# Attention inside a fused kernel: small vector operations rewritten as sums beside a constant, gates moved to other factors, one copy moved to VectorE, and a new order of the rounds

## The chip, the core and the metric

The kernel runs on one core of a Trainium2 chip. A core has TensorE for matrix products and transpositions (PE in the profile; PEld is its loading of weights), VectorE (DVE), ScalarE (ACT), GpSimd (POOL) and a queue (SP) that issues most of the DMA transfers. The metric is the time of one execution in microseconds, the median over several runs.

## The reference

Three stages follow one another: an attention with a memory, a dense layer with a layer norm inside, and a gated dense layer. Only the first is changed.

```python
# B, H, S, D = 4, 8, 576, 64
scores = q @ k.T / sqrt(D), causal; scores -= scores.max(-1)
a = np.exp(scores); a /= a.sum(-1, keepdims=True) + 1e-09
local = a @ v
q_p = phi(q)                       # phi(x) = (x if x > 0 else exp(x) - 1) + 1
mem_ret = q_p @ M_prev
mem_norm = (q_p @ z_prev)[..., None] + 1e-06
g = 1 / (1 + exp(-beta))           # one gate per head
attn = g * mem_ret / mem_norm + (1 - g) * local
# then, over 2304 tokens:
x = layer_norm(softmax-gated(attn @ w_in)) @ w_out      # _moe_ref
out = (sigmoid(x @ w_gate) * (x @ w_val)) @ w_out2      # _moe2_ref
```

## The kernel before

The attention works on 16 pairs of heads (4 batches, 4 pairs each, so that two heads of width 64 fill 128 partitions). The 576 rows of a pair are four blocks of 128 and a tail of 64, which for both heads together makes a fifth block; so a pair has nine row groups (two heads in each of four blocks, and the tail), and its transformed q has ten columns of 64.

One pair goes through these steps, which the text calls by the names of their methods:

- `lq`, `lk`, `lv`, `lz`: loads of q, k, v with M, and z. `tq_p`, `tk_p`: q and k are transposed on TensorE; `tq_h`, `tk_h` (ScalarE) round them to a high part and `tq_l`, `tk_l` (VectorE) form the rest.
- `ph_e` (ScalarE), `ph_m` (VectorE, lines 306 and 307), `ph_g` (GpSimd, line 311, writes `G`), `ph_r` (VectorE, lines 321 to 323, writes `nr`), `ph_s` (GpSimd, line 328): phi(q), its product with z, the sums of ten blocks of 64 as normalisers, and phi(q) divided by them. `tf_p` and `tf_c` transpose the result and copy it out.
- `s0` to `s4`: for each block `s_p` (TensorE, scores), `s_m` (VectorE, line 378, mask and row maximum), `s_e` (ScalarE, line 386, exponential, which also writes the row sums). `n01_r`, `n23_r`, `n4_r` (VectorE, lines 390 and 391, write `rs`) invert the row sums, and `n0_p` to `n4_p` (GpSimd, line 395) multiply the rows by them.
- `g0`, `g1`, `t0` to `t3`, `tt`, `tc`: transpositions of the probabilities (`_p`, TensorE) and copies out of PSUM (`_c`). `x0_m`, `a00`, `a01` and `x1_m`, `a10` to `a14`: the products that give the output, copied into `X` by `x0_c` and `x1_c`.

Beside each pair a sixteenth of the first dense layer's weights, which come as 64-bit numbers, is converted: `cv_a` (VectorE, lines 108 and 109), `cv_r` (ScalarE), `cv_b` (VectorE, lines 117 and 122), `cv_p` (GpSimd, line 502), `cv_h` (ScalarE), `cv_l` (VectorE, line 510).

The order is written out by hand in `ORDER`: one round runs through the whole list, and `name:d` means that round i does this step for pair i+d. Within an engine the instructions stand in that order; between engines only data and buffers make one wait for another. Score tiles in PSUM share two buffers, as do the transposed probabilities. The second and third stage are ordered by a scheduler, not by this list.

The gates enter twice before the change: `g10` holds 1 + exp(-beta), by which the normalisers are multiplied before they are inverted, and `o9` holds 1/(1-g), by which the row sums are multiplied before they are inverted.

Of the kernel before, what the change touches and what calls it, by code (L numbers as in the profile page):

```python
# [22 lines left out]
tk_p:1 cv_a:-1 tq_h:1 n01_r:0 ph_g:1 tq_l:1 t1_p:-1 tk_h:1 cv_r:-1 t2_p:-1 tk_l:1 t2_c:-1 n0_p:0 t1_c:-1 cv_b:-1
n4_r:0 x0_m:-1 a01:-1 a00:-1 x1_m:-1 a14:-1 a13:-1 a12:-1 a11:-1 a10:-1 s0_p:1 s3_e:0 n1_p:0 s1_p:1 ph_r:1 s2_e:0
cv_p:-1 n4_p:0 s0_m:1 lq:3 lv:0 cv_h:-1 s1_m:1 s2_p:1 n23_r:0 s3_p:1 g0_p:0 tt_p:0 lk:3 ph_s:1 s2_m:1 lz:3 cv_d:0
s4_p:1 x1_c:-1 s0_e:1 s1_e:1 tt_c:0 g0_c:0 s3_m:1 tf_p:1 x0_c:-1 tc_p:0 g1_p:0
# [831 lines left out]
```

## Time and profile before

| What | Value |
|---|---|
| median of three runs | 920.97 us (920.97 to 921.63) |
| the profiled execution | 921.52 us, of which 919.7 us are the span shown |
| PE busy over the span | 870.2 us (95%) |
| DVE busy | 578.1 us (63%) |
| ACT busy | 423.8 us (46%) |
| POOL busy | 260.1 us (28%) |

The attention takes about the first 243 us. The shares are averages over stages that differ: a stage is read from its own windows and timelines. Times in a timeline row are the start in us and the busy time in us; a number in brackets is the idle time of that engine just before and what ended it. Where rows are merged (x4), the busy time is that of the group.

### The profile page before, as it was taken

Reading aid. Unit: us, or ns where it says so; the run is one execution under the profiler, and the core shown is the slowest. Engines: PE = TensorE matmul, PEld = TensorE weight load, DVE = VectorE, ACT = ScalarE, POOL = GpSimd, SP = SyncE. Lnnn points to the kernel's source line nnn. Section 1 sums busy time; section 2 is a strip of 40 time slices with the busy share of each in tenths; the row PEclk is TensorE's granted clock in tenths of the full one; section 3 lists DMA queues with packets and bytes.
Section 4 is the critical chain, followed back from the end, with each engine's and each line's share of the span. In section 5 each row is a group of like instructions: output and inputs, shape, how many; then the busy total and the mean of one; then the engine's idle time right before and its main releaser. Section 6 shows DMA issues by size and latency. Waiting matters only on the chain.

```text
span 919.7 us, 13972 instructions
## 1 busy us (share of the span) xinstructions
PE 870.2 (95%) x5224; PEld 723.4 (79%) x5224; DVE 578.1 (63%) x1321; ACT 423.8 (46%) x941; POOL 260.1 (28%) x320
## 2 busy tenths in 40 slices
PE   3799898998988999999999999999999999999998
PEld 3566666666667999999988888888888888888887
DVE  5899999999596755574924248456339735232324
ACT  2788988897676654554435233112122212111111
POOL 2566656666574211111400033012014203000000
PEclk9899999999998999999999999999999999999999
DMA  4333433442122100020300013002002300000113
GB/s 89 87 93 93 108 85 90 104 94 83 47 68 69 47 18 29 24 69 1 114 25 1 1 46 109 29 17 76 1 1 92 91 1 1 1 1 1 46 46 115
DMA packets 76292, 48.63 MB, mean 53 GB/s; under 512 B 62656, under 2 KB 62656, under 8 KB 76224
## 3 DMA queue, kind: packets, MB, share of 16 engines
q1 hardware_dynamic: 75024, 47.44, 18.6%
q8 instruction: 41, 0.67, 0.3%
q10 hardware_dynamic: 1200, 0.30, 0.2%
q14 instruction: 27, 0.22, 0.1%
HBM read 43.00 MB, written 4.72 MB: 52 GB/s over the span
## 4 chain that ended last, share of the span: by engine, by line
PE 69%; ACT 15%; DVE 7%; POOL 5%; issue 3%; DMA 1%; SPq 0%; POOLq 0%; DVEq 0%; ACTq 0%
PE gv L736 32%; PE po L755 16%; PE po L654 9%; PE h L603 7%; ACT p L386 6%; POOL p L395 3%; ACT Bt L135 2%; ACT q L280 1%; PE pl L642 1%; ACT E L300 1%; ACT kh L135 1%; ACT f L135 1%; PE sc L356 1%; PE x L465 1%; DVE exwo L109 1%
## 5 line engine op out<-in xcount | busy, mean ns | idle before, releaser
L742 DVE TENSOR_TENSOR sg<-sg,gv 128x512 f32<-128x512 f32 (+1 forms) x60 | 38.0, 633 | 176.8 <-ACT sg L741 176.8
L741 ACT ACTIVATE sg<-gv 128x512 f32<-128x512 f32 (+1 forms) x60 | 33.2, 554 | 234.6 <-PE gv L736 234.6
L736 PE MATMUL gv<-xx,gh 128*128 128x512 f32 (+1 forms) x480 | 136.1, 368 | 0.2 <-ACT xx L138 0.2
L736 PE MATMUL gv<-xx,vh 128*128 128x512 f32 (+1 forms) x480 | 136.0, 368 | 0.0
L654 PE MATMUL po<-lnT,woh 128*128 128x256 f32 x576 | 106.5, 287 | 0.3 <-ACT X L658 0.3
L736 PEld LDWEIGHTS gv<-xx,gh 128*128 128x128 f32 x480 | 87.4, 188 | 16.1 <-issue 0.4
L736 PEld LDWEIGHTS gv<-xx,vh 128*128 128x128 f32 x480 | 87.1, 189 | 14.9
L654 PEld LDWEIGHTS po<-lnT,woh 128*128 128x128 f32 x576 | 91.7, 194 | 1.4 <-ACT X L658 0.5
L736 PE MATMUL gv<-xx,gl 128*128 128x512 f32 (+1 forms) x240 | 88.3, 368 | 0.0
L736 PE MATMUL gv<-xx,vl 128*128 128x512 f32 (+1 forms) x240 | 88.3, 368 | 0.0
L386 ACT ACTIVATE p<-p,nm 128x128 f32<-128x128 f32 (+2 forms) x144 | 83.0, 585 | 7.0 <-DVE nm L378 7.0
L395 POOL TENSOR_SCALAR p<-p,rs 128x128 f32<-128x128 f32 (+2 forms) x144 | 78.5, 563 | 20.0 <-DVE rs L391 13.3
L755 PE MATMUL po<-oh,GVxs 128*128 128x512 f32 x216 | 84.1, 389 | 0.0
L755 PE MATMUL po<-ol,GVxs 128*128 128x512 f32 x216 | 84.1, 389 | 0.0
L755 PE MATMUL po<-oh,GVe 128*128 128x512 f32 x216 | 84.0, 389 | 0.0
L654 PE MATMUL po<-lnT,wol 128*128 128x256 f32 x288 | 81.8, 285 | 0.0
L603 PE MATMUL h<-wih,xs 128*128 128x512 f32 x288 | 80.6, 393 | 0.0
L762 DVE TENSOR_TENSOR X<-X,po 128x512 f32<-128x512 f32 x90 | 61.3, 684 | 22.9 <-PE po L755 22.9
L603 PEld LDWEIGHTS h<-wih,xs 128*128 128x128 f32 x288 | 53.0, 188 | 10.6 <-issue 0.5
L356 PE MATMUL sc<-kh,q 64*128 64x128 f32 (+3 forms) x256 | 37.2, 376 | 25.2 <-DVE nm L378 17.9
L142 POOL TENSOR_SCALAR gh<-exg 128x512 fp32r<-128x512 f32 x12 | 8.9, 749 | 183.0 <-PE gv L736 142.1
L138 ACT CAST GVxs<-sg 128x512 fp32r<-128x512 f32 (+1 forms) x60 | 34.8, 580 | 46.5 <-DVE sg L742 46.5
(355 smaller groups left out, 1802.2 us busy)
## 6 DMA issues: line engine op xcount, KB each, us to landing
rawg<-in_moe_w_gate_dram SPq DMA_DIRECT2D x12, 512.0 KB, 3.8
rawv<-in_moe_w_val_dram SPq DMA_DIRECT2D x12, 512.0 KB, 3.9
rawo<-in_moe_w_out_dram SPq DMA_DIRECT2D x12, 512.0 KB, 3.5
out_dram<-X SPq DMA_DIRECT2D x18, 256.0 KB, 2.0
qt<-in_q_dram SPq DMA_DIRECT2D x32, 128.0 KB, 2.8
vt<-in_v_dram SPq DMA_DIRECT2D x32, 128.0 KB, 2.9
raw<-in_moe_w_in_dram SPq DMA_DIRECT2D x16, 256.0 KB, 3.6
rawwo<-in_moe_w_out_dram SPq DMA_DIRECT2D x8, 512.0 KB, 3.5
```

The costliest lines, as they stand in the source:

```text
L135: (nc.scalar.copy if COPY[key] == "s" else nc.vector.tensor_copy)(dst, src)
L138: nc.scalar.copy(hi, src)
L356: nc.tensor.matmul(ps[:, hh, :w], q2[sl, c, w - P : w], kk[sl, :w], start=m == 0, stop=m == 2)
L386: nc.scalar.activation(p, p, AF.Exp, bias=nm, scale=-1.0, accum_out=r["sum"][:, c : c + 1])
L395: nc.gpsimd.tensor_scalar(p, p, r["rs"][:, c : c + 1], 1.0, ALU.mult, ALU.mult)
L603: nc.tensor.matmul(ph[:, j * 512 : j * 512 + 512], xs[:, s, c], w[:, j * 512 : j * 512 + 512], start=(c == 0 and s == 0 and w is hi), stop ...
L654: nc.tensor.matmul(po[:, :GW], w[:, m * P : m * P + P], L[:, x, c], start=(c == 0 and n == 0), stop=(c == NF1 - 1 and n == 2),)
L736: nc.tensor.matmul(ps[:, j, :w], wt[:, c, fs], xx[:, x, c], start=(c == 0 and n == 0), stop=(c == NC - 1 and n == 2),)
L741: nc.scalar.activation(sg[:, :w], ps[:, 0, :w], AF.Sigmoid)
L742: nc.vector.tensor_mul(sg[:, :w], sg[:, :w], ps[:, 1, :w])
L755: nc.tensor.matmul(po, GV[x][:, f, sl], wt[:, f], start=(f == 0 and n == 0), stop=(f == NCH - 1 and n == 2),)
L762: nc.vector.tensor_add(acc[:, t], acc[:, t], po)
```

## The change

Four things are changed in the attention.

1. `G` becomes one fixed tile with 65 columns for each of the ten blocks; the 65th holds 1e-6, so that one reduction gives normaliser plus constant, and the operation on line 322 that added 1e-6 and multiplied by the gate is gone. The row sums likewise go to a fixed tile with a second column of 1e-9, and the operation on line 390 becomes a reduction over two columns.
2. The gates become factors: g multiplies in `tf_c` as the scale of a ScalarE activation, and 1-g is the second factor of the GpSimd multiplication in `n_p`, whose second factor was the constant 1.0. The tables `g10` and the inverse of `o9` are not built any more.
3. `x1_c`, a copy of 128x320 elements out of PSUM, goes from ScalarE to VectorE.
4. `ORDER` is new, k of the first pair comes over the SP queue like the others (before, over ScalarE's queue), and beta is loaded first of all, one round earlier.

```diff
-s4_m:0 n3_p:-1 tq_p:1 ph_e:1 tf_c:0 tc_c:-1 g1_c:-1 t3_p:-1 s4_e:0 n2_p:-1 cv_l:-2 t0_p:-1 ph_m:1 t3_c:-1 t0_c:-1
...
+t3_c:-1 tq_p:1 n1_p:0 t0_c:-1 x1_c:-2 lq:2 tq_h:1 cv_a:-1 t2_p:-1 t1_p:-1 ph_m:1 t2_c:-1 s4_e:0 tk_p:1 ph_g:1
...
-COPY = dict(tf="s", tc="v", tt="s", kh="s", x0="v", x1="s", g0="s", g1="v", t0="s", t1="s", t2="s", t3="s")
+COPY = dict(tc="v", tt="s", kh="s", x0="v", x1="v", g0="s", g1="v", t0="s", t1="s", t2="s", t3="s")
...
+            self.G = sb.tile([P, 10, D + 1], F32, tag="G", name="G")
+            nc.vector.memset(self.G[:, :, D:], 1e-6)
+            self.sum = [sb.tile([P, 9, 2], F32, tag=f"sum{n}", name=f"sum{n}") for n in range(2)]
+            for t in self.sum:
+                nc.vector.memset(t[:, :, 1:], 1e-9)
...
-            nc.vector.tensor_scalar(bt, bt, 1.0, 1e30, ALU.add, ALU.min)
+            nc.vector.tensor_scalar_add(bt, bt, 1.0)
+            nc.vector.reciprocal(bt, bt)
             bth = bt.rearrange("p (a h) -> p a h", h=2)
-            self.g10 = sb.tile([P, HP, 10], F32, tag="g10", name="g10")
-            for c in range(NB + 1):
-                nc.vector.tensor_copy(self.g10[:, :, 2 * c : 2 * c + 2], bth)
-            nc.vector.reciprocal(bt, bt)
...
-            nc.vector.tensor_scalar_max(self.o9, self.o9, 1e-30)
-            nc.vector.reciprocal(self.o9, self.o9)
...
-            self.load_qk(n, self.kt[n % 2], k, nc.sync.dma_start if n else nc.scalar.dma_start)
+            self.load_qk(n, self.kt[n % 2], k)
...
-            nc.vector.reduce_sum(nr, r["G"].rearrange("p (c d) -> p c d", d=D), axis=AX.X)
-            nc.vector.scalar_tensor_tensor(nr, nr, 1e-6, self.g10[:, pairs[n][1]], ALU.add, ALU.mult)
+            nc.vector.reduce_sum(nr, self.G, axis=AX.X)
             nc.vector.reciprocal(nr, nr)
...
-            copy("tf", r["f"], r["fps"])
+            hp = pairs[n][1]
+            nc.scalar.mul(r["f"], r["fps"], self.gp[:, hp : hp + 1])
...
-            rs, sm, o9 = (x[:, c0:c1] for x in (r["rs"], r["sum"], self.o9[:, pairs[n][1]]))
-            nc.vector.scalar_tensor_tensor(rs, sm, 1e-9, o9, ALU.add, ALU.mult)
+            rs = r["rs"][:, c0:c1]
+            nc.vector.reduce_sum(rs, self.sum[n % 2][:, c0:c1], axis=AX.X)
             nc.vector.reciprocal(rs, rs)
...
-                nc.gpsimd.tensor_scalar(p, p, r["rs"][:, c : c + 1], 1.0, ALU.mult, ALU.mult)
+                og = self.o9[:, pairs[n][1], c : c + 1]
+                nc.gpsimd.tensor_scalar(p, p, r["rs"][:, c : c + 1], og, ALU.mult, ALU.mult)
...
-                if it == -1:
+                if it == -2:
                     self.gates_load()
```

VectorE's order in a round in the middle of the attention, from the last row maximum of pair 7 (tile `p_119`) to the first use of pair 8's q. `wil` is the weight conversion's last step, `ex` and `raw` belong to its first, `X` is the output, `E` is phi(q), `C` and `A` are transposed probabilities. Before:

```order
L378 ISA p_119,nm<-sc_4_1670,mask 128x576
L378 ISA nm 128x1
L135 COPY C_1719<-t6d 128x128
L135 COPY A_1686<-t6a_1702 128x2x128
L510 TENSOR_TENSOR wil_77<-ex_1531,wih_76 128x256
L306 TENSOR_SCALAR E_1715<-E_1715 128x640
L307 SCALAR_TENSOR_TENSOR E_1715<-qt_92,E_1715 128x640
L108 TENSOR_SCALAR ex_1744<-raw_1668 128x256
L109 TENSOR_SCALAR ex_1744<-raw_1668 128x256
L390 SCALAR_TENSOR_TENSOR rs_1679<-sum_1678,o_200 128x4
L391 RECIPROCAL rs_1679<-rs_1679 128x4
```

Here lines 306 and 307 come first and lines 108 and 109 directly behind them. After the change, around the same place:

```order
L388 TENSOR_REDUCE rs_1605<-sum_126 128x4
L389 RECIPROCAL rs_1605<-rs_1605 128x4
L135 COPY C_1675<-t6d 128x128
L509 TENSOR_TENSOR wil_77<-ex_1501,wih_76 128x256
L377 ISA p_119,nm<-sc_4_1680,mask 128x576
L377 ISA nm 128x1
L135 COPY X<-x_1_1545 128x5x64
L108 TENSOR_SCALAR ex_1713<-raw_1657 128x256
L109 TENSOR_SCALAR ex_1713<-raw_1657 128x256
L306 TENSOR_SCALAR E_1694<-E_1694 128x640
L307 SCALAR_TENSOR_TENSOR E_1694<-qt_92,E_1694 128x640
```

Lines 108 and 109 now stand ahead of lines 306 and 307, not behind them; the copy of 128x5x64 into `X` stands here; and the inversion of the row sums of blocks 0 and 1 has moved ahead of the last maximum.

GpSimd's order over one whole round, beginning with the product that writes `G`. Before:

```order
L311 TENSOR_TENSOR G_1324<-E_1287,zm_599 128x640
L395 TENSOR_SCALAR p_0_1186<-p_0_1186,rs_1251 128x128 x2
L395 TENSOR_SCALAR p_1_1200<-p_1_1200,rs_1251 128x256 x2
L502 TENSOR_TENSOR ex_1316<-ex_1316 128x256
L395 TENSOR_SCALAR p_119<-p_119,rs_1251 128x576
L328 TENSOR_TENSOR E_1287<-E_1287,nr_1391 128x640
L395 TENSOR_SCALAR p_3_1260<-p_3_1260,rs_1251 128x512 x2
L395 TENSOR_SCALAR p_2_1235<-p_2_1235,rs_1251 128x384 x2
```

Here the row groups of blocks 0 and 1 follow the product, and those of blocks 3 and 2 close the round. After:

```order
L310 TENSOR_TENSOR G<-E_1272,zm_778 128x10x64
L394 TENSOR_SCALAR p_119<-p_119,rs_1185,o_196 128x576
L394 TENSOR_SCALAR p_0_1172<-p_0_1172,rs_1185,o_196 128x128 x2
L501 TENSOR_TENSOR ex_1291<-ex_1291 128x256
L326 TENSOR_TENSOR E_1272<-E_1272,nr_1372 128x640
L394 TENSOR_SCALAR p_3_1221<-p_3_1221,rs_1185,o_196 128x512 x2
L394 TENSOR_SCALAR p_2_1200<-p_2_1200,rs_1185,o_196 128x384 x2
L394 TENSOR_SCALAR p_1_1390<-p_1_1390,rs_1395,o_196 128x256 x2
```

The row groups of blocks 3, 2 and 1 (`p_3`, `p_2`, `p_1`) now stand directly ahead of the product that writes `G`, and the tail's group and block 0 directly behind it.

On TensorE the transposition of phi(q) (`tf_p`) now stands ahead of the tail's scores (`s4_p`), so that these use the PSUM buffer of the fourth block's scores and wait for its maximum. In the second stage the scheduler's order differs too at its beginning: the first transposition of that stage's results (line 642) stood behind three row tiles' products on line 603 and now stands behind three and three quarters; the second stood two more tiles later and now stands a quarter of a tile later.

## Rows read from the trace of the kernel before

**Rows 1.** Windows: busy us (count) of PE, PEld, DVE, ACT, POOL; clock, DMA share, GB/s.

```profile
120.00:140.00 20.00, 17.98 (x163) 12.48 (x162) 19.55 (x62) 18.50 (x53) 13.16 (x20) 1.00 0.43 99
300.00:400.00 100.00, 100.00 (x673) 92.14 (x673) 62.62 (x137) 55.63 (x97) 17.18 (x21) 1.00 0.12 38
```

**Rows 2.** Timeline of DVE, one round: start, busy, line, operation, tiles.

```profile
119.64 1.66 DVE L109 TENSOR_SCALAR ex<-raw 128x256 int32<-128x256 int32 x1
...
124.18 0.80 DVE L321 TENSOR_REDUCE nr<-G 128x10 f32<-128x640 f32 x1
125.02 0.60 DVE L322 SCALAR_TENSOR_TENSOR nr<-nr,g 128x10 f32<-128x10 f32 x1
...
126.84 0.48 DVE L390 SCALAR_TENSOR_TENSOR rs<-sum,o 128x4 f32<-128x4 f32 x1
...
129.60 0.42 DVE L135 COPY X<-x 128x256 f32<-128x256 f32 x1
...
133.08 1.66 DVE L109 TENSOR_SCALAR ex<-raw 128x256 int32<-128x256 int32 x1
```

**Rows 3.** Timeline of POOL, the same round.

```profile
119.60 1.55 POOL L311 TENSOR_TENSOR G<-E,zm 128x640 f32<-128x640 f32 x1 [2.84 <-DVE E L307]
121.76 1.64 POOL L395 TENSOR_SCALAR p<-p,rs 128x128 f32<-128x128 f32 x4 [0.60 <-DVE rs L391]
124.15 0.73 POOL L502 TENSOR_TENSOR ex<-ex 128x256 f32<-128x256 f32 x1 [0.75 <-DVE rs L390]
124.86 0.75 POOL L395 TENSOR_SCALAR p<-p,rs 128x576 f32<-128x576 f32 x1
126.05 1.26 POOL L328 TENSOR_TENSOR E<-E,nr 128x640 f32<-128x640 f32 x1 [0.44 <-DVE nm L378]
127.71 2.50 POOL L395 TENSOR_SCALAR p<-p,rs 128x512 f32<-128x512 f32 x4 [0.40 <-ACT p L386]
```

**Rows 4.** Timeline of DVE: three of these operations at other times.

```profile
17.63 0.17 DVE L322 SCALAR_TENSOR_TENSOR nr<-nr,g 128x10 f32<-128x10 f32 x1
...
25.45 0.15 DVE L390 SCALAR_TENSOR_TENSOR rs<-sum,o 128x4 f32<-128x4 f32 x1
...
229.52 0.29 DVE L109 TENSOR_SCALAR ex<-raw 128x256 int32<-128x256 int32 x1
```

**Rows 5.** Timeline of PE, the same round.

```profile
126.29 0.62 PE L356 MATMUL sc<-kh,q 64*128 64x384 f32 x4 [0.84 <-DVE nm L378]
...
128.72 0.51 PE L347 MATMUL sc<-kh,q 128*128 128x288 f32 x2
...
129.47 0.30 PE L347 MATMUL sc<-kl,q 128*128 128x288 f32 x1
...
133.00 1.15 PE L417 MATMUL t7b<-ident,p 128*128 128x128 f32 x8 [0.26 <-ACT Bt L135]
```

**Rows 6.** Timeline of ACT, the same round.

```profile
125.96 0.42 ACT L135 COPY X<-x 128x320 f32<-128x320 f32 x1
...
129.00 0.59 ACT L135 COPY Bt<-t7c 128x512 f32<-128x512 f32 x1 [0.85 <-PE t7c L431]
...
130.66 0.74 ACT L300 ACTIVATE E<-qt 128x640 f32<-128x640 f32 x1 [0.58 <-POOL p L395]
```

**Rows 7.** Timeline of ACT, the beginning.

```profile
10.42 0.21 ACT L302 ACTIVATE bt<-bt 128x8 f32<-128x8 f32 x1 [2.53 <-DMA bt<-in_beta_dram]
```

**Rows 8.** Timeline of DVE, the beginning.

```profile
15.38 0.17 DVE L801 TENSOR_SCALAR gl<-gl 128x8 f32<-128x8 f32 x1 [1.23 <-DMA gl<-in_moe_g_ln_dram]
```

**Rows 9.** Timeline of POOL: `G` of pairs 2 and 15.

```profile
38.96 1.55 POOL L311 TENSOR_TENSOR G<-E,zm 128x640 f32<-128x640 f32 x1 [4.86 <-DVE E L307]
...
214.78 1.55 POOL L311 TENSOR_TENSOR G<-E,zm 128x640 f32<-128x640 f32 x1 [2.83 <-DVE E L307]
```

**Rows 10.** Timeline of PE, the two longest waits of the second stage's beginning.

```profile
262.76 1.09 PE L642 MATMUL pl<-ident,e 128*128 128x128 f32 x8 [2.32 <-ACT e L625]
...
280.66 1.12 PE L642 MATMUL pl<-ident,e 128*128 128x128 f32 x4 [3.82 <-DVE lnT L139]
```

More of the change, by code (lines that the diff above doesn't have):

```diff
@@ L21 @@
 ORDER = """
-s4_m:0 n3_p:-1 tq_p:1 ph_e:1 tf_c:0 tc_c:-1 g1_c:-1 t3_p:-1 s4_e:0 n2_p:-1 cv_l:-2 t0_p:-1 ph_m:1 t3_c:-1 t0_c:-1
[L23 to L26, printed above, removed]
+t3_c:-1 tq_p:1 n1_p:0 t0_c:-1 x1_c:-2 lq:2 tq_h:1 cv_a:-1 t2_p:-1 t1_p:-1 ph_m:1 t2_c:-1 s4_e:0 tk_p:1 ph_g:1
+tk_h:1 tq_l:1 cv_r:-1 n4_r:0 tk_l:1 t1_c:-1 n4_p:0 x0_m:-1 a01:-1 a00:-1 x1_m:-1 a14:-1 a13:-1 a12:-1 a11:-1 a10:-1
+lv:0 s0_p:1 s2_e:0 s1_p:1 g1_p:0 ph_r:1 n0_p:0 s3_e:0 cv_b:-1 x0_c:-1 s0_m:1 lk:2 s1_m:1 s0_e:1 s2_p:1 cv_p:-1
+g1_c:0 n23_r:0 lz:2 s2_m:1 s3_p:1 g0_p:0 ph_s:1 s1_e:1 g0_c:0 s3_m:1 tt_p:0 n3_p:0 n2_p:0 cv_d:0 tf_p:1 t3_p:0
+tt_c:0 n01_r:1 cv_h:-1 tc_p:0 tc_c:0 cv_l:-1 tf_c:1 s4_p:1 t0_p:0 s4_m:1 ph_e:2
 """.split()
-COPY = dict(tf="s", tc="v", tt="s", kh="s", x0="v", x1="s", g0="s", g1="v", t0="s", t1="s", t2="s", t3="s")
+COPY = dict(tc="v", tt="s", kh="s", x0="v", x1="v", g0="s", g1="v", t0="s", t1="s", t2="s", t3="s")
 CVL = "v"
@@ L215, in gates, with load_qk @@
             nc.vector.tensor_scalar(self.o9[:, :, 8], self.gp, -1.0, 1.0, ALU.mult, ALU.add)
-            nc.vector.tensor_scalar_max(self.o9, self.o9, 1e-30)
-            nc.vector.reciprocal(self.o9, self.o9)
         def psum(self, shape, name, tag="s"):
             return self.ps.tile(shape, F32, tag=tag, name=name, bufs=2)
-        def load_qk(self, n, t, src, dma=nc.sync.dma_start):
+        def load_qk(self, n, t, src):
             b, hp = pairs[n]
             for hh in range(2):
-                dma(
+                nc.sync.dma_start(
                     t[:, : 8 * D].rearrange("p (c h d) -> p c h d", h=2, d=D)[:, :, hh],
@@ L229, in load_qk @@
                 )
-            dma(
+            nc.sync.dma_start(
                 t[0:64, 8 * D : 10 * D].rearrange("p (h d) -> p h d", h=2),
@@ L309, in ph_g @@
         def ph_g(self, n, r):
-            r["G"] = self.sb.tile([P, 10 * D], F32, tag="G", name=f"G{n}")
             nc.gpsimd.tensor_mul(
-                r["G"].rearrange("p (c x) -> p c x", x=P),
-                r["E"].rearrange("p (c x) -> p c x", x=P),
-                r["z"].unsqueeze(1).to_broadcast([P, NB + 1, P]),
+                self.G[:, :, :D].rearrange("p (c h) d -> p c h d", h=2),
+                r["E"].rearrange("p (c h d) -> p c h d", h=2, d=D),
+                r["z"].rearrange("p (h d) -> p h d", h=2).unsqueeze(1).to_broadcast([P, NB + 1, 2, D]),
             )
@@ L381, in s_e @@
         def s_e(self, n, r, i):
-            if "sum" not in r:
-                r["sum"] = self.sb.tile([P, 9], F32, tag="sum", name=f"sum{n}", bufs=2)
+            if "rs" not in r:
                 r["rs"] = self.sb.tile([P, 9], F32, tag="rs", name=f"rs{n}", bufs=2)
             for (_, _, _, p, c), nm in zip(self.parts(r, i), r["m", i]):
-                nc.scalar.activation(p, p, AF.Exp, bias=nm, scale=-1.0, accum_out=r["sum"][:, c : c + 1])
+                nc.scalar.activation(p, p, AF.Exp, bias=nm, scale=-1.0, accum_out=self.sum[n % 2][:, c, 0:1])
         def n_r(self, n, r, c0, c1):
-            rs, sm, o9 = (x[:, c0:c1] for x in (r["rs"], r["sum"], self.o9[:, pairs[n][1]]))
-            nc.vector.scalar_tensor_tensor(rs, sm, 1e-9, o9, ALU.add, ALU.mult)
+            rs = r["rs"][:, c0:c1]
+            nc.vector.reduce_sum(rs, self.sum[n % 2][:, c0:c1], axis=AX.X)
             nc.vector.reciprocal(rs, rs)
```

## The prediction, made before the changed kernel had run

> **What bounds the kernel now.** I read the windows by stage first, then the timelines of one round on VectorE, GpSimd, TensorE and ScalarE side by side. In the middle of the attention VectorE is busy 19.55 of 20 us, TensorE 17.98, ScalarE 18.50; from 300 us on TensorE is busy all of the time and VectorE 63% [rows 1]. So a small VectorE operation can only matter in the attention, where it is worth its time once per round. A round lasts 13.44 us, from line 109 at 119.64 to line 109 at 133.08 [rows 2], and VectorE has no gap in it that the timeline marks.
>
> But three of its busy times are not work. Line 109 takes 1.66 us here and 0.29 us at 229.52; line 322 takes 0.60 and at 17.63 only 0.17; line 390, for blocks 2 and 3, takes 0.48 and at 25.45 only 0.15 [rows 2, 4]. Each ends when a GpSimd operation ends: line 109 at 121.30, `G` at 121.15; line 322 at 125.62, the tail's group at 124.86 + 0.75 = 125.61; line 390 at 127.32, phi(q) times its normaliser at 126.05 + 1.26 = 127.31 [rows 2, 3]. The hold costs 1.37 + 0.43 + 0.33 = 2.13 us per round, and VectorE's own work is 13.44 - 2.13 = 11.31 us. The reduction on line 321 reads one tensor and takes 0.80 us.
>
> The Trainium skill gives this hold as a rule (SBUF — State Buffer, Who interferes with whom): a VectorE instruction with two SBUF inputs, or in a two-port mode, and a GpSimd instruction exclude one another for a whole instruction, while `tensor_reduce` on trn2 never contends. The three pairs of ends agree with the first half; that a reduction is never held the trace does not show for two columns. By the rule the new reductions are free of the hold; without it they would keep 0.43 + 0.33 us.
>
> **The change part by part.** *Line 322 goes*: 0.17 us of work, and 0.43 of hold. *Line 390 becomes a reduction over two columns*, three times a round. No row shows one so small; the reduction of 640 elements at 0.80 us is the bound above, 0.15 us the nearest row by size [rows 2, 4]. I take 0.15, that is no change in work, and 0.33 of hold gone; it could be 0.15 dearer each, or 0.1 cheaper. The longer row of `G` (650 for 640) is 0.01 us.
>
> *`x1_c` moves to VectorE*: the copy of 256 columns takes 0.42 us there [rows 2], so 320 take between 0.42 and 0.53; I take 0.45. It leaves ScalarE, where it took 0.42 [rows 6]. VectorE's work is then 11.31 - 0.17 + 0.01 + 0.45 = 11.60 us.
>
> *The new order* decides the 1.37 us of line 109. Before, it stands right behind line 307, whose end releases `G` on GpSimd, and so meets `G` in every round. Now it stands ahead of line 306, at a time when GpSimd should have finished the row groups of block 1 and waits for line 307: the hold is gone. GpSimd has the room: 1.55 + 1.64 + 0.73 + 0.75 + 1.26 + 2.50 = 8.43 us of work in a round [rows 3]. But holds can appear elsewhere: lines 117 and 122 now come when GpSimd multiplies block 0, and line 510 when it multiplies blocks 2 and 1. Each can cost at most the rest of one such operation, 0 to 0.75 us [rows 3]; I take 0.3 for all. A second term: the tail's scores now wait for block 3's maximum. They take 128.72 to 129.47 + 0.30 = 1.05 us on TensorE [rows 5], and VectorE has meanwhile only an inversion, the copy of `C` and line 510 before it needs them. I take 0.3 us of wait, between 0 and 1.05. That makes 11.60 + 0.3 + 0.3 = 12.2 us.
>
> What is late next: TensorE is busy 17.98/20 x 13.44 = 12.1 us of a round [rows 1], with waits of 0.84 and 0.26 in it [rows 5]; ScalarE has gaps of 0.85 and 0.58 [rows 6], so 13.44 - 1.43 = 12.0 us of work, less 0.42 for the copy, 11.6. Three engines within half a microsecond of each other will miss some handshakes; I add 0.2 and take a round of 12.4 us, with 11.9 and 13.0 as ends. The gate as a scale in `tf_c` and the second per-partition factor in `n_p` I cost at nothing: both fall on engines with some slack, ScalarE 0.8 us and GpSimd 4 us a round. Where that cover is gone is rival E.
>
> `G` of pair 2 starts at 38.96 and of pair 15 at 214.78 [rows 9]: 13 rounds. They save 13 x (13.44 - 12.4) = 13.5 us. The round after that is bound by VectorE for some three quarters: 0.8.
>
> *The start.* beta is loaded after two pairs' q and k before; ScalarE waits 2.53 us for it, with the rounding of q queued behind [rows 7], and that wait goes. VectorE waits 1.23 us for `gl` ahead of the first normalisers [rows 8]; the scheduler now puts this after the row maxima of pair 0, so it goes too, or shrinks. Seven small operations that built `g10` and inverted `o9` go, at some 0.17 each [rows 4, 8] 1.2 us. Against these 5.0 us: beta's issue stands ahead of q's, and k of the first pair comes behind q on one queue, where its rounding waits for that of q anyway. I take 4.0, between 1 and 5.
>
> *The second stage* keeps its work; its order at the beginning differs. TensorE waits there 2.32 and 3.82 us before transpositions [rows 10]. The first one gets three quarters of a row tile of products ahead of it, which covers its wait; the second comes much sooner after it and should wait longer. I take 0, with 4 us either way.
>
> Sum: 13.5 + 0.8 + 4.0 = 18.3 us. The profiled execution has 921.52 us: 921.5 - 18.3 = 903.2. The median of the runs is 0.55 below it, less than a third of a per cent, so I say **903 us**.
>
> **The rivals.** *B, the holds only change place.* The new rows of GpSimd meet lines 117, 122 and 510, and perhaps line 109 again if block 1 runs late. Speaking for it: GpSimd works 8.43 us of every round and VectorE still has eight operations a round that it can hold. Against it: the longest meeting, with `G`, is taken apart by the order. Then a round is 13.0: 14 x 0.44 + 4 = 10 us, 911 us. The skill's sentence "Issue order, not op shape, decides who blocks" (same page and section) is this rival's rule; the ends above agree, since the same line takes 0.29 or 1.66.
>
> *C, more is gained.* If the tail's wait and the new holds both come to nothing, VectorE's 11.6 and TensorE's 12.1 less what hides in it allow 11.9: 14 x 1.54 + 5 = 26.6 us, 895 us. Against it: the two waits have their places in the order.
>
> *D, the round does not change.* If ScalarE's chain of copies and exponentials, 11.6 us without any wait, meets two waits as long as today's, 1.43, and the held 0.3 on top, a round is 13.3 again. Only the start remains, and up to that much can be lost in the second stage: 917 to 921, here 920.
>
> *E, slower.* GpSimd's multiplication gets a second per-partition factor where a constant stood; the trace has no such form. The nine of a round take 1.64 + 0.75 + 2.50 = 4.89 us [rows 3]. If each cost twice that, GpSimd would work 13.3 us, and its waits at handovers, 0.60 + 0.75 + 0.44 + 0.40 = 2.19 [rows 3], come on top: 15.5 us a round, 14 x 2.1 - 4 = 25 us more, 946 us. It decides from 13.44 - 8.43 - 2.19 = 2.8 us on, that is from 58% dearer. Against it: the first factor is per partition already.
>
> **How the numbers follow.** Forecast (897 to 909 us) 0.57, B 0.21, C 0.11, D 0.06, E 0.05. Within 0.2%, or 1.8 us, a measurement of this kernel can hardly tell a change; D lies mostly there. Faster: 0.57 + 0.21 + 0.11 + 0.02 of D = 0.91; within 0.2%: 0.04; slower: 0.05. The range must reach well into B and into C: 895 to 914 leaves out D, E and the ends of B and C, just under 2 in 10.
>
> **What would show it.** In the profile after: line 109 at about 0.3 us in the rounds; reductions of two columns at about 0.15; starts of `G` 12.4 us apart, and `G` of pair 2 some 4 us earlier; VectorE waiting briefly for TensorE before the tail's maximum; GpSimd's multiplications as long as before. It would be wrong if line 109, 117 or 510 are held for over half a microsecond in each round, if the two-factor multiplication is much longer, or if the second stage's first 60 us have lost what the attention won.

## The result, and the profile after

The changed kernel takes **900.18 us** (median of four runs, 899.37 to 901.93) where the kernel before takes 920.97: a ratio of 0.9777, with a 95% interval of 0.976 to 0.9794. Forecast were 903.0, within 895 to 914. The profiled execution has a span of 898.4 us, 21.3 less than before. Line numbers are lower by one or two than before: `G` is written on line 310, `nr` on 320 and 321, `rs` on 388 and 389, the row groups are multiplied on 394, the maxima taken on 377; lines 108, 109, 117 and 122 have kept theirs, and line 510 is now 509.

The windows of the kernel after, same columns as [rows 1]:

```profile
120.00:140.00 20.00, 20.00 (x175) 14.38 (x172) 19.32 (x72) 19.04 (x57) 16.19 (x23) 1.00 0.48 112
300.00:400.00 100.00, 100.00 (x663) 91.56 (x662) 57.53 (x125) 54.82 (x92) 15.33 (x19) 1.00 0.11 32
```

TensorE, which had 17.98 of 20 us, now has all of them, and VectorE is nearly as busy as before: the bound of a round has passed from one to the other, with little between them. From 300 us on TensorE is busy all of the time, as before.

VectorE's timeline over one round of the kernel after, which answers to [rows 2]:

```profile
120.99 0.82 DVE L320 TENSOR_REDUCE nr<-G 128x10 f32<-128x650 f32 x1
...
121.98 0.52 DVE L117 SCALAR_TENSOR_TENSOR ex<-raw,ex 128x256 int32<-128x256 int32 x1
...
126.96 0.15 DVE L388 TENSOR_REDUCE rs<-sum 128x4 f32<-128x8 f32 x1
...
127.63 0.52 DVE L509 TENSOR_TENSOR wil<-ex,wih 128x256 fp32r<-128x256 f32 x1
128.23 0.76 DVE L377 CUSTOM_DVE_ANT_1 p<-sc,mask 128x576 f32<-128x576 f32 x1
...
128.91 0.49 DVE L135 COPY X<-x 128x320 f32<-128x320 f32 x1
...
129.51 0.29 DVE L109 TENSOR_SCALAR ex<-raw 128x256 int32<-128x256 int32 x1
```

Line 109 is at 0.29 us instead of 1.66, and the reduction over two columns takes 0.15 us in the middle of GpSimd's multiplications (125.07 to 129.11, below). GpSimd over the same round, beside [rows 3]:

```profile
119.02 1.55 POOL L310 TENSOR_TENSOR G<-E,zm 128x640 f32<-128x640 f32 x1 [2.03 <-DVE E L307]
...
125.07 4.04 POOL L394 TENSOR_SCALAR p<-p,rs,o 128x512 f32<-128x512 f32 x6
131.15 1.55 POOL L310 TENSOR_TENSOR G<-E,zm 128x640 f32<-128x640 f32 x1 [2.03 <-DVE E L307]
```

From `G` to `G` a round is 12.13 us; it was 13.44. `G` of pairs 2 and 15 after, beside [rows 9]:

```profile
33.80 1.56 POOL L310 TENSOR_TENSOR G<-E,zm 128x640 f32<-128x640 f32 x1 [2.66 <-DVE E L307]
...
192.69 1.56 POOL L310 TENSOR_TENSOR G<-E,zm 128x640 f32<-128x640 f32 x1 [1.86 <-DVE E L307]
```

With [rows 9] this splits the 21.3 us: up to `G` of pair 2 the kernel gains 38.96 - 33.80 = 5.2; in the 13 rounds to pair 15 (214.78 - 38.96) - (192.69 - 33.80) = 175.82 - 158.89 = 16.9; behind that it loses 0.8 (705.7 us to the end against 704.9).

VectorE at the beginning, beside [rows 8], and TensorE's long waits early in the second stage, beside [rows 10]:

```profile
19.64 0.17 DVE L800 TENSOR_SCALAR gl<-gl 128x8 f32<-128x8 f32 x1 [2.58 <-DMA gl<-in_moe_g_ln_dram]
```

```profile
238.28 0.70 PE L602 MATMUL h<-wih,xs 128*128 128x512 f32 x2 [2.47 <-DVE e L615]
...
247.09 2.11 PE L641 MATMUL pl<-ident,e 128*128 128x128 f32 x8 [2.19 <-ACT e L624]
252.19 0.80 PE L653 MATMUL po<-lnT,woh 128*128 128x256 f32 x2 [2.99 <-DVE lnT L139]
```

The wait for `gl` has not gone but doubled, from 1.23 to 2.58 us. The second stage waits at other places than before and for about as long: these three waits add up to 7.65 us, and the two of [rows 10], with a third of 0.98 between them, to 7.12.

### The profile page after: what moved, and what is told of

It reads as the page before. It is cut to its first block, busy times and chain, and to the rows that moved or that the text cites. A ratio compares the mean times of both kernels' runs of the same rounds, so it can differ in the third digit from the quotient of the medians.

```text
span 898.4 us, 13966 instructions
## 1 busy us (share of the span) xinstructions
PE 869.9 (97%) x5224; PEld 724.4 (81%) x5224; DVE 555.1 (62%) x1317; ACT 419.4 (47%) x925; POOL 273.1 (30%) x320
## 4 chain that ended last, share of the span: by engine, by line
PE 88%; DVE 6%; POOL 2%; issue 1%; DMA 1%; ACT 1%; SPq 0%; POOLq 0%; DVEq 0%; ACTq 0%
PE gv L735 33%; PE po L754 16%; PE po L653 9%; PE h L602 7%; PE x L464 5%; PE sc L355 4%; PE x L449 2%; PE sc L346 1%; PE pl L641 1%; PE trk L265 1%; PE trq L265 1%; PE trf L265 1%; DVE hm L609 1%; DVE exwo L119 1%; DVE exwo L108 1%
## 5 line engine op out<-in xcount | busy, mean ns | idle before, releaser
L394 POOL TENSOR_SCALAR p<-p,rs,o 128x256 f32<-128x256 f32 (+2 forms) x144 | 91.8, 652 | 11.6 <-ACT q L280 6.1
L653 PEld LDWEIGHTS po<-lnT,wol 128*128 128x128 f32 x288 | 56.0, 195 | 0.2
```

Of the source, the lines that this page charges most:

```text
L394: nc.gpsimd.tensor_scalar(p, p, r["rs"][:, c : c + 1], og, ALU.mult, ALU.mult)
L653: nc.tensor.matmul(po[:, :GW], w[:, m * P : m * P + P], L[:, x, c], start=(c == 0 and n == 0), stop=(c == NF1 - 1 and n == 2),)
```

## The experiments

Two questions were open: which part of the change shortens the rounds, and what the stretch behind the rounds depends on. All rounds below are distances from one start of `G` to the next.

**1. The new arithmetic alone.** The changed kernel with the order, the loads and the copy of before:

```diff
-t3_c:-1 tq_p:1 n1_p:0 t0_c:-1 x1_c:-2 lq:2 tq_h:1 cv_a:-1 t2_p:-1 t1_p:-1 ph_m:1 t2_c:-1 s4_e:0 tk_p:1 ph_g:1
+s4_m:0 n3_p:-1 tq_p:1 ph_e:1 tf_c:0 tc_c:-1 g1_c:-1 t3_p:-1 s4_e:0 n2_p:-1 cv_l:-2 t0_p:-1 ph_m:1 t3_c:-1 t0_c:-1
...
-COPY = dict(tc="v", tt="s", kh="s", x0="v", x1="v", g0="s", g1="v", t0="s", t1="s", t2="s", t3="s")
+COPY = dict(tc="v", tt="s", kh="s", x0="v", x1="s", g0="s", g1="v", t0="s", t1="s", t2="s", t3="s")
```

> The new arithmetic alone (reductions beside a constant, gates as factors), with the order, the loads and the copies of the kernel before. Theory 1 (the rounds gained what VectorE was held by GpSimd, each hold by its own cause): the reductions of two columns take 0.15 us and are not held, line 109 keeps its 1.4 us of hold, since it still stands behind line 307. A round is 13.44 - 0.17 - 0.43 - 0.33 = 12.5 us (12.4 to 12.8), the time 921 - 13 x 0.9 - 1 = 908 us (904 to 911). Theory 2 (the holds only move: what is freed is taken by another instruction): round 13.2 or more, 916 us or more. Theory 3 (the gain is the new order's alone, the arithmetic costs GpSimd time): round 13.4, 920 us.

909.09 us (907.13 to 909.80), a ratio of 0.9871 (0.9855 to 0.9886); the round is 12.87. VectorE, then GpSimd:

```profile
125.65 1.66 DVE L109 TENSOR_SCALAR ex<-raw 128x256 int32<-128x256 int32 x1
127.23 0.15 DVE L388 TENSOR_REDUCE rs<-sum 128x4 f32<-128x8 f32 x1
...
129.26 0.73 DVE L117 SCALAR_TENSOR_TENSOR ex<-raw,ex 128x256 int32<-128x256 int32 x1
```

```profile
118.32 0.82 POOL L394 TENSOR_SCALAR p<-p,rs,o 128x576 f32<-128x576 f32 x1
```

The reductions are free and line 109 stays held, as theory 1 has it. But the round gains 0.57 us and not 0.9: line 117 takes 0.73 here, 0.31 more than in the kernel before, so theory 2 has a share too. Line 117 there:

```profile
123.25 0.42 DVE L117 SCALAR_TENSOR_TENSOR ex<-raw,ex 128x256 int32<-128x256 int32 x1
```

The round of 12.87 lies outside theory 1's range. That the time lies inside it is luck: 13 rounds gained 7.4 us instead of 12, and the start made up for the larger part, with `G` of pair 2 at 35.47, 3.5 us earlier than before, where 1 was expected. GpSimd's multiplication with two factors takes 0.82 us for 576 columns where it took 0.75 [rows 3]: a tenth dearer, not the 58% from which rival E decides.

**2. One entry of the order alone.** The kernel before, lines 108 and 109 ahead of 306 and 307:

```diff
-... cv_l:-2 t0_p:-1 ph_m:1 t3_c:-1 t0_c:-1
-tk_p:1 cv_a:-1 tq_h:1 ...
+... cv_l:-2 t0_p:-1 cv_a:-1 ph_m:1 t3_c:-1
+t0_c:-1 tk_p:1 tq_h:1 ...
```

> The kernel before with one entry of the order moved: lines 108 and 109 ahead of lines 306 and 307. Theory 1: line 109 falls from 1.66 to 0.29 us, the holds of lines 322 and 390 stay; a round is 13.44 - 1.37 = 12.1 by VectorE alone, with TensorE's 12.1 us beside it 12.2 to 12.6, the time some 907 us (904 to 911). Theory 2: lines 322, 390, 117 or 510 are held longer for it, round 13.0 or more, 914 us or more. Theory 3 (order as a whole): one entry moves little, within 3 us of 921.

916.89 us (915.35 to 918.56), 0.9961 (0.9947 to 0.9975): 4 us, where theory 1 expected 14. VectorE at three places of this trace:

```profile
105.64 0.29 DVE L108 TENSOR_SCALAR ex<-raw 128x256 int32<-128x256 int32 x1 [2.81 <-DMA raw<-in_moe_w_in_dram]
105.85 0.29 DVE L109 TENSOR_SCALAR ex<-raw 128x256 int32<-128x256 int32 x1
...
126.69 0.48 DVE L322 SCALAR_TENSOR_TENSOR nr<-nr,g 128x10 f32<-128x10 f32 x1
...
128.40 0.49 DVE L390 SCALAR_TENSOR_TENSOR rs<-sum,o 128x4 f32<-128x4 f32 x1
...
135.86 1.05 DVE L284 SCALAR_TENSOR_TENSOR q<-trq,q 128x512 fp32r<-128x512 f32 x3 [0.51 <-ACT q L280]
```

Line 109 is free in every round, and the undisturbed rounds take 12.97 us. That is 0.47 less than before, of the 1.37 that line 109 no longer takes: lines 322 and 390 stay held, and VectorE now waits 0.51 us for ScalarE's rounding of q. And in six rounds line 108 waits for the raw weights, up to 2.8 us: in the order of before they are asked for some 6 us ahead of their use, behind q, v and k (the first at 32.40, used at 38.79). The entry could not be moved alone; the new order also asks for them 16 us ahead (15.87, used at 31.96).

**3. Both, with the earlier load.** Experiment 1 with the entry moved and the raw weights loaded a round earlier:

```diff
-... cv_l:-2 t0_p:-1 ph_m:1 t3_c:-1 t0_c:-1
-tk_p:1 cv_a:-1 tq_h:1 ...
-... s2_m:1 lz:3 cv_d:0
+... cv_l:-2 t0_p:-1 cv_a:-1 ph_m:1 t3_c:-1
+t0_c:-1 tk_p:1 tq_h:1 ...
+s2_m:1 lz:3 cv_d:1 ...
```

> The kernel before with the new arithmetic, lines 108 and 109 ahead of lines 306 and 307, and the raw weights loaded one round earlier, so that line 108 does not wait for them; the rest of the order, the loads of the start and the copy on ScalarE as before. Theory 1 (all three holds of a round go, and nothing else of the new order is needed): VectorE 11.2 to 11.6 us, TensorE 12.1 and its waits: a round of 12.1 to 12.4, the time 904 to 907 us (the gain at the start and of the second stage is left out). Theory 2 (the holds move to lines 117, 122 and 510): 12.7 or more, 910 us or more.

906.79 us (906.28 to 906.90), 0.9845 (0.983 to 0.986); the round is 12.63, between the two theories. The time lies in theory 1's range by luck: 13 rounds gained 10.7 us, and the other 4.5 came from the start (`G` of pair 2 at 37.73) and from behind pair 15 (701.6 us instead of 704.9), which the expectation had left out. VectorE:

```profile
124.97 0.29 DVE L109 TENSOR_SCALAR ex<-raw 128x256 int32<-128x256 int32 x1
...
127.41 1.05 DVE L284 SCALAR_TENSOR_TENSOR q<-trq,q 128x512 fp32r<-128x512 f32 x3 [0.61 <-ACT q L280]
...
129.17 0.65 DVE L117 SCALAR_TENSOR_TENSOR ex<-raw,ex 128x256 int32<-128x256 int32 x1
```

All three old holds are gone, and two things have come: VectorE waits 0.61 us for ScalarE's rounding of q, and line 117 is held 0.23. The other half microsecond of the change, from 12.63 to 12.13, needs the rest of the order and the copy.

**4. The changed kernel with that one entry moved back.**

```diff
-t3_c:-1 tq_p:1 n1_p:0 t0_c:-1 x1_c:-2 lq:2 tq_h:1 cv_a:-1 t2_p:-1 t1_p:-1 ph_m:1 t2_c:-1 s4_e:0 tk_p:1 ph_g:1
+t3_c:-1 tq_p:1 n1_p:0 t0_c:-1 x1_c:-2 lq:2 tq_h:1 t2_p:-1 t1_p:-1 ph_m:1 cv_a:-1 t2_c:-1 s4_e:0 tk_p:1 ph_g:1
```

> The changed kernel with the same one entry moved back: lines 108 and 109 directly behind lines 306 and 307. Theory 1: line 109 is held again until G ends, 1.6 to 1.7 us; VectorE, 11.7 us of work in a round of 12.13, has 0.4 us to spare, so that about 1.0 us of the 1.4 shows: a round of 13.0 to 13.3, 911 to 916 us. Theory 2 (deeper overlap of the new order, holds don't matter): line 109 is long, but the round stays at 12.2, 900 to 902 us.

920.69 us (916.64 to 923.23), 0.9989 (0.9973 to 1.0004): with one entry the whole gain is gone, more than either theory allowed. VectorE, then GpSimd:

```profile
127.69 1.65 DVE L109 TENSOR_SCALAR ex<-raw 128x256 int32<-128x256 int32 x1
...
141.13 0.30 DVE L109 TENSOR_SCALAR ex<-raw 128x256 int32<-128x256 int32 x1
```

```profile
127.64 1.56 POOL L310 TENSOR_TENSOR G<-E,zm 128x640 f32<-128x640 f32 x1 [1.63 <-DVE E L307]
...
141.09 1.77 POOL L310 TENSOR_TENSOR G<-E,zm 128x640 f32<-128x640 f32 x1 [1.63 <-DVE E L307]
...
153.16 1.55 POOL L310 TENSOR_TENSOR G<-E,zm 128x640 f32<-128x640 f32 x1 [1.62 <-DVE E L307]
```

These rows are an experiment inside the experiment. In the round that starts at 127.64 `G` wins, line 109 takes 1.65 us and the round 13.45. At 141.09 VectorE wins: line 109 takes 0.30, `G` takes 1.77 instead of 1.56, and the round 12.07. So with the same two instructions either can lose: the loser waits, for 1.35 us if it is VectorE, for 0.21 if it is GpSimd, and the round shows all of it. The Trainium skill has the rule that issue order and not the shape of an operation decides who blocks (SBUF — State Buffer, Who interferes with whom). The rows agree that the shape does not decide it; the issue order they can't show, since `G` starts 0.05 us ahead of line 109 where line 109 loses and 0.04 ahead where it wins. My allowance that 0.4 us of the hold would find cover was wrong.

The profiled execution is the fastest of the ten: its 13 rounds lose 14.1 us against the changed kernel, and the stretch behind pair 15 another 2.4. The other nine take 0.6 to 6.6 us longer than it, eight of them at a mean granted clock of 0.983 to 0.987 where it has 0.989; how much of that lies in the rounds no trace shows.

**5. The new order with the old arithmetic.** The kernel before with the order, the loads and the copy on VectorE of the changed one:

```diff
-COPY = dict(tf="s", tc="v", tt="s", kh="s", x0="v", x1="s", g0="s", g1="v", t0="s", t1="s", t2="s", t3="s")
+COPY = dict(tf="s", tc="v", tt="s", kh="s", x0="v", x1="v", g0="s", g1="v", t0="s", t1="s", t2="s", t3="s")
...
-            self.load_qk(n, self.kt[n % 2], k, nc.sync.dma_start if n else nc.scalar.dma_start)
+            self.load_qk(n, self.kt[n % 2], k)
...
-                if it == -1:
+                if it == -2:
```

> The order, the loads and the copy on VectorE of the changed kernel, with the arithmetic of the kernel before (lines 322 and 390 as operations with two inputs and a scalar, f copied, one factor in GpSimd's multiplications). Theory 1 (each hold by its own cause): line 109 is free (0.29 us), lines 322 and 390 meet GpSimd's row groups again and are held some 0.3 to 0.4 us each; VectorE's 11.7 us of the changed kernel gets 0.17 and 0.5 to 0.8 more: a round of 12.4 to 12.7, the time 904 to 908 us. Theory 2 (the order alone brings it all): 12.1 to 12.2 a round, 899 to 902 us.

910.52 us (910.09 to 912.74), 0.9895 (0.9878 to 0.9911); the round is 12.90. Both are above theory 1's ranges, and further from theory 2's. VectorE:

```profile
128.24 0.66 DVE L390 SCALAR_TENSOR_TENSOR rs<-sum,o 128x1 f32<-128x1 f32 x1
...
130.64 0.17 DVE L322 SCALAR_TENSOR_TENSOR nr<-nr,g 128x10 f32<-128x10 f32 x1
...
133.37 0.41 DVE L390 SCALAR_TENSOR_TENSOR rs<-sum,o 128x4 f32<-128x4 f32 x1
...
138.59 0.28 DVE L109 TENSOR_SCALAR ex<-raw 128x256 int32<-128x256 int32 x1
```

Line 322 happens to be free in this order, but line 390 is held twice, by 0.51 and 0.26 us over its 0.15. In the new order the new arithmetic is therefore worth 0.77 us a round (12.90 to 12.13), in the old one 0.57. Theory 2, that the order alone brings it all, fails; theory 1 has the kind of hold right, but a round 0.2 too short. TensorE is busy for 19.54 of 20 us here and VectorE for 18.95 (120 to 140 us), so what bounds this round is not settled.

**6. The copy back on ScalarE** in the changed kernel:

```diff
-COPY = dict(tc="v", tt="s", kh="s", x0="v", x1="v", g0="s", g1="v", t0="s", t1="s", t2="s", t3="s")
+COPY = dict(tc="v", tt="s", kh="s", x0="v", x1="s", g0="s", g1="v", t0="s", t1="s", t2="s", t3="s")
```

> The changed kernel with the copy x1_c back on ScalarE (0.42 us there, 0.49 on VectorE). Theory 1 (TensorE sets the round at 12.1 us): the round stays at 12.1 to 12.2 and the time within 1.5 us of 900.2. Rival (ScalarE's relief is what brought the round from 12.5 to 12.1): round 12.4 or more, 904 us or more. Rival (VectorE still sets the round): 11.7 us, 894 us.

898.60 us (898.22 to 898.79), 0.9761 (0.9745 to 0.9777). The windows of this kernel:

```profile
120.00:140.00 20.00, 19.49 (x175) 13.51 (x174) 18.25 (x66) 19.59 (x58) 14.94 (x19) 1.00 0.43 99
```

The round is 12.34: TensorE has half a microsecond of 20 free and ScalarE next to none. The copy on VectorE is worth 0.2 us a round, 2 us in 13 rounds (160.9 against 158.9); theory 1 had expected none, and its rival more. And yet the median is 1.6 us lower than the changed kernel's (the intervals of the two ratios overlap), and in the profiled execution the stretch behind `G` of pair 15 takes 701.1 us instead of 705.7. None of the theories had that.

**7. More work for TensorE in each round.** The 128x128 transposition of the tail's corner done five times:

```diff
-            nc.tensor.transpose(r["tc"], self.p4[n % 2][:, S0:], ident)
+            for _ in range(5):
+                nc.tensor.transpose(r["tc"], self.p4[n % 2][:, S0:], ident)
```

> The changed kernel with the transposition of the tail's corner (tc_p, 128x128) done five times into the same place instead of once: four more on TensorE in each round, at 0.14 us each by the rate of eight in 1.15 us, that is 0.57 us. Theory (TensorE sets the round of 12.13 us): a round of 12.6 to 12.7, the time 907 to 909 us. Rival (VectorE or ScalarE sets it and TensorE only looks busy): a round of 12.1 to 12.3, 900 to 903 us.

904.63 us (901.93 to 905.29), 0.9817 (0.9801 to 0.9833). The transposition in the changed kernel, then in this one; then this kernel's window and GpSimd:

```profile
127.05 0.33 PE L437 MATMUL t8d<-ident,p 128*128 128x128 f32 x1
```

```profile
130.41 0.77 PE L438 MATMUL t8d<-ident,p 128*128 128x128 f32 x5
```

```profile
120.00:140.00 20.00, 20.00 (x181) 14.57 (x181) 19.04 (x66) 19.21 (x55) 13.52 (x18) 1.00 0.39 90
```

```profile
122.37 1.56 POOL L310 TENSOR_TENSOR G<-E,zm 128x640 f32<-128x640 f32 x1 [2.47 <-DVE E L307]
...
134.93 1.56 POOL L310 TENSOR_TENSOR G<-E,zm 128x640 f32<-128x640 f32 x1 [2.47 <-DVE E L307]
```

The round grows by 0.43 us to 12.56, which is what the five take over the one (0.77 us against 0.33), and TensorE stays busy for 20 of 20: TensorE does set the round. The 0.57 us expected were too many. The time grows by 4.5 us, less than the 5.5 of 13 rounds: in the profiled execution, at 901.93 the fastest of the four, the stretch behind pair 15 takes 701.5 us, 4.2 less than in the changed kernel, though the second stage runs through nearly the same order.

**8. `gl` earlier.** Loaded behind beta and scaled among the gates:

```diff
             nc.sync.dma_start(self.bt, beta.unsqueeze(0).to_broadcast([P, H]))
+            nc.sync.dma_start(gl, moe_g_ln.rearrange("(c p) -> p c", p=P))
...
+            nc.vector.tensor_scalar_mul(gl, gl, 2.0**-20)
             nc.vector.tensor_scalar_add(bt, bt, 1.0)
...
-    nc.sync.dma_start(gl, moe_g_ln.rearrange("(c p) -> p c", p=P))
-    nc.vector.tensor_scalar_mul(gl, gl, 2.0**-20)
```

> The changed kernel with the scale vector gl loaded right behind beta and scaled among the gates, so that VectorE does not wait 2.58 us for it between the inversions of the row sums of pair 0. Theory: G of pairs 1 and 2 come 1.5 to 2.5 us earlier, the rounds stay, the time falls to 898 to 899 us. Rival (another wait of the start ends just as late, TensorE's for scores of pair 0 or the loads of pair 1): G of pair 2 within 0.5 us, 900 us.

903.97 us (903.17 to 904.98), 0.9816 (0.9801 to 0.9831): slower than the changed kernel by some 4 us, which neither theory had. The rounds are the same, `G` of pair 2 comes at 33.25, 0.55 us earlier than in the changed kernel; so the wait of 2.58 us had mostly other waits beside it. Behind pair 15 the kernel takes 711.0 us. TensorE in the second stage:

```profile
273.13 0.75 PE L655 MATMUL po<-lnT,woh 128*128 128x256 f32 x4 [1.45 <-ACT woh L582]
275.45 0.58 PE L655 MATMUL po<-lnT,wol 128*128 128x256 f32 x1 [1.57 <-POOL wol L145]
```

Two waits have come, for the conversion of the second matrix, where the changed kernel has 0.58 us.

**What the stretch behind the rounds depends on.** Where one kernel differed from another there, the granted clock and TensorE's idle time did. The windows of 100 us from about `G` of pair 15 on, first of the changed kernel, then of 8 (`gl`), of 7 (more work), of 6 (copy on ScalarE); the third number from the end is the clock:

```profile
192.00:292.00 100.00, 89.06 (x522) 70.59 (x522) 69.70 (x157) 65.73 (x127) 52.70 (x54) 0.93 0.18 61
```

```profile
192.00:292.00 100.00, 86.71 (x489) 67.90 (x486) 69.25 (x160) 64.66 (x124) 52.58 (x54) 0.90 0.19 61
```

```profile
198.00:298.00 100.00, 91.00 (x567) 73.14 (x568) 71.37 (x166) 68.50 (x133) 53.26 (x54) 0.98 0.19 61
```

```profile
195.00:295.00 100.00, 91.20 (x564) 74.28 (x561) 75.28 (x168) 71.85 (x139) 52.46 (x55) 0.97 0.19 61
```

All kernels, one profiled execution each, in the 100 us from about their own `G` of pair 15 on:

| Kernel | clock | TensorE not busy, us | us behind `G` of pair 15 |
|---|---|---|---|
| 10, copy on ScalarE in the last pair | 0.97 | 8.6 | 700.8 |
| 6, copy on ScalarE | 0.97 | 8.8 | 701.1 |
| 7, more work | 0.98 | 9.0 | 701.5 |
| 3, arithmetic and entry | 0.97 | 8.8 | 701.6 |
| 2, entry alone | 0.97 | 9.7 | 702.5 |
| 9, more work in the last pair | 0.95 | 8.3 | 703.2 |
| 5, order | 0.95 | 9.2 | 703.2 |
| 1, arithmetic | 0.97 | 10.6 | 703.6 |
| before | 0.95 | 11.0 | 704.9 |
| after | 0.93 | 10.9 | 705.7 |
| 4, entry moved back | 0.91 | 11.2 | 708.1 |
| 8, `gl` earlier | 0.90 | 13.3 | 711.0 |

In these traces the clock is either 1.00 (2.4 GHz) or 0.50 (1.2 GHz), and the falls of this stretch come in or behind TensorE's waits. A hundredth over 100 us is a microsecond of products at full speed. From kernel 10 to kernel 8 the clock makes 7 us and the idle time 4.7, of a spread of 10.2; the two overlap, since a low clock costs nothing while TensorE is idle. This is a comparison of kernels and not yet a cause: the same waits make TensorE idle and precede the falls. And single executions of one kernel do not always follow their mean clock: two of the changed kernel at 0.989 take 899.37 and 901.93 us.

**9. The clock, tried by itself.** The extra transpositions of experiment 7 in the last pair only; on every engine the order is that of the changed kernel but for these four instructions:

```diff
-            nc.tensor.transpose(r["tc"], self.p4[n % 2][:, S0:], ident)
+            for _ in range(5 if n == NP - 1 else 1):
+                nc.tensor.transpose(r["tc"], self.p4[n % 2][:, S0:], ident)
```

> The changed kernel with the transposition of the tail's corner done five times instead of once in the last pair alone; nothing else moves on any engine, and TensorE has 0.57 us more work, at the end of the attention, where it waits 0.57, 0.42 and 0.44 us one after the other. In the changed kernel the granted clock falls there from 1.00 to 0.50 (212 to 217 us) and again from 246 to 257 us. Theory (the rest behind the rounds differs between the kernels by how often TensorE's waits bring the clock to its lower level, 1.7 us each time, and the waits of the end of the attention are one such place): no fall at 212, the rest behind G of pair 15 is 704 us or less instead of 705.7, the time 896 to 899 us, although there is more work. Rival (the clock follows something else): the fall stays, 900 to 901.5 us.

898.80 us (898.70 to 899.76), 0.9765 (0.9751 to 0.9779). The windows at that place, of the changed kernel and of this one:

```profile
210.00:220.00 10.00, 8.72 (x55) 5.50 (x55) 4.03 (x11) 3.91 (x9) 3.12 (x5) 0.83 0.01 2
```

```profile
210.00:220.00 10.00, 8.68 (x65) 5.66 (x65) 4.32 (x15) 4.66 (x11) 3.54 (x5) 1.00 0.01 2
```

With more work the fall at 212 is gone, and the stretch behind pair 15 is 703.2 us, 2.5 less. The median is 1.4 us lower; the intervals of the two ratios overlap. But two things keep this from showing the clock as the cause. First, only part of the 2.5 us lies where the fall was. TensorE in this kernel, to be held against the rows of the changed kernel under the profile after:

```profile
237.96 1.07 PE L603 MATMUL h<-wih,xs 128*128 128x512 f32 x2 [2.47 <-DVE e L616]
...
250.88 0.79 PE L654 MATMUL po<-lnT,woh 128*128 128x256 f32 x2 [0.55 <-DVE lnT L139]
```

From `G` of pair 15 to the wait of 2.47 us the kernel gains 1.2 us (45.6 to 44.4); behind it, the wait before `po` falls from 2.99 to 0.55 us, with every engine's order the same. Second, the fall can stay away without added work. Kernel 10, below, has the order of the changed kernel at this place; both wait 0.57 and 0.42 us, and then, the changed kernel first:

```profile
212.04 2.63 PE L416 MATMUL t15b<-ident,p 128*128 128x128 f32 x12 [0.44 <-ACT Bt L135]
```

```profile
213.19 1.27 PE L416 MATMUL t15b<-ident,p 128*128 128x128 f32 x8 [0.45 <-ACT Bt L135]
```

```profile
213.00:218.00 5.00, 4.57 (x42) 3.15 (x44) 3.18 (x10) 2.71 (x7) 1.26 (x2) 1.00 0.00 0
```

The last row is kernel 10's window: its clock stays at 1.00, and its twelve transpositions take 1.27 and 0.66 us with a wait of 0.24 between, where they take 2.63 in the changed kernel. So the rows show what a fall costs, but not that the four transpositions prevented it; with one trace of each kernel that stays open.

**10. The two put together.** The copy on ScalarE for the last pair alone, which gives the second stage the order of experiment 6 and leaves the rounds:

```diff
-            copy(
-                f"x{g}", X[:, t0 : t0 + w // 64, hp],
+            (nc.scalar.copy if g == 1 and n >= 15 else nc.vector.tensor_copy)(
+                X[:, t0 : t0 + w // 64, hp],
```

> The changed kernel with the copy x1_c on ScalarE for the last pair alone. Every engine's order in the second and third stage is then that of the kernel with all these copies on ScalarE (span behind G of pair 15: 701.1 us, against 705.7 in the changed kernel), and the rounds are those of the changed kernel (13 rounds in 158.9 us, against 160.9). Theory (the rounds are TensorE's, the rest is the second stage's order with its waits and falls of the clock, and the two add): 893 to 897 us, less than any kernel so far. Rival (with the copies on ScalarE the rounds themselves bring the better end): 900 us, with the rest at 705 to 706.

**896.75 us** (896.45 to 897.04), a ratio of 0.974 (0.9726 to 0.9753), which lies wholly below that of the changed kernel. 13 rounds take 158.9 us and the rest 700.8: the terms add, as the theory has it. This kernel has the lowest median of all; its interval and that of 6 overlap.

## Why the prediction was right

Its terms, one by one.

- *The holds* were the mechanism. Line 109: experiment 4 shows its 1.37 us whole, in rounds of 13.45 and 12.07; in the old order, where other holds and waits stand behind it, its removal brought 0.47 (2). Lines 322 and 390: the reductions run at 0.15 us in the midst of GpSimd's work, and the new arithmetic is worth 0.57 us a round in the old order (1) and 0.77 in the new (5), where I had 0.76 of hold and 0.17 of work.
- *The round* was forecast at 12.4, between 11.9 and 13.0, and is 12.13. The step that was mis-sized is the sum of 0.3 for new holds, 0.3 for the tail's wait and 0.2 for near ties on top of VectorE's 11.6. The holds are 0.10 each on lines 117 and 509 (0.52 us where each takes 0.42 in the kernel before), the tail's maximum starts 0.08 us behind the end of line 509 (127.63 + 0.52 to 128.23), and the ties cost nothing that the timeline marks. So VectorE is busy for 19.32 of 20 us, 11.7 of a round, just under TensorE's 12.1, and that, which stood in the prediction as what is late next, is the round (7). Over 13 rounds 0.27 us make the 3.4 by which they gained more than forecast (16.9 for 13.5).
- *The copy* takes 0.49 us where I took 0.45. In the sum it stood as a cost to VectorE, the engine taken for the bound; it brings 0.2 us a round, since ScalarE is the third engine at its limit (6).
- *The order* was credited with taking line 109 out of `G`'s way. True, but only because the raw weights are asked for earlier as well: on the old order the same move ran into their load (2). The prediction did not look at that queue.
- *GpSimd's second factor*, costed at nothing, takes a tenth more time per multiplication; its wait ahead of `G` fell from 2.84 to 2.03 us [rows 3], and that slack covers it. Rival E falls with that. The gate as a scale in `tf_c`, also costed at nothing, takes ScalarE 0.76 us where the copy took 0.62; ScalarE, busy for 19.04 of 20 us without the moved copy, has room for it.
- *The start* was put at 4.0 and measured at 5.2; kernels 9 and 10, with the same attention, have `G` of pair 2 at 34.62 and 34.93, which is 4.3 and 4.0. Within that scatter the size was right. Its parts are not shown: the new arithmetic with the old loads starts `G` of pair 2 3.5 us earlier than before (1), where the seven operations stood at 1.2, but only 1.2 earlier in kernel 3, and the new order and loads with the old arithmetic 1.9 earlier (5). The wait for beta is gone, as the prediction had it. The sentence that the wait for `gl` goes or shrinks was wrong: it doubled. It cost little where it stands (8).
- *Behind `G` of pair 15* the sum had 0.8 for the last round and 0 for the second stage with 4 either way; measured is a loss of 0.8, so 1.6 less than forecast. The reason given, the length of two waits, was only a part of it: a new wait of 2.47 us came, and the granted clock, which the prediction did not treat, goes with this stretch as much as the waits do.

So the sum of 18.3 us met 21.3 in the profiled execution with errors of +3.4 in the rounds, +1.2 at the start and -1.6 behind them. That they partly cancel is luck.

Rival B (holds only change place) has a real share in the old order, where line 117 took on 0.31 and 0.23 us (1, 3), and nearly none in the new. Rival C's round of 11.9 is excluded by TensorE's 12.1, busy all of the time. D and E are refuted: the round fell by 1.3 us, and GpSimd's multiplications are a tenth dearer.

What stays open: why `G` of pair 2 starts up to 1.1 us apart in kernels whose beginnings are alike; what decides whether the clock falls at one place in kernels of one order (9, 10); and whether the wide scatter of experiment 4 comes from how often VectorE wins (its one trace shows it winning in 2 rounds of 13) or from the clock, which was lower in most of its slower executions.

## What to carry to other kernels

When VectorE looks full, compare the durations of one line between a crowded and an empty stretch: here the surplus was waiting for GpSimd, and it could be removed by form (a reduction) or by order (ahead of the operation that releases GpSimd). How much of it the round returns has to be measured: all of 1.37 us in the new order (4), 0.47 of it in the old (2). Before moving an instruction ahead, look at when its data was asked for. Where TensorE is the bound, look at its waits and at the granted clock behind them together: a change upstream that cost 2 us in the rounds came with 4.6 us less behind them, where the scheduler had made another order (6).
